# Low parts of the weights on VectorE, two attention tiles on the later path, and block 1 in two pieces for four triples

## The chip, the cores and the metric

One NeuronCore of one Trainium2 chip runs the kernel. The metric is the device time of one execution in microseconds (us); the median of three runs is compared. Engines: TensorE (PE; its weight loads are PEld), VectorE (DVE), ScalarE (ACT), GpSimd (POOL), SyncE (SP), which issues the transfers.

## The reference

Attention in chunks, then two gated layers over all 3072 tokens (4 batches of 768), all in float32 and with weights handed over as 64-bit floats:

```python
for c in range(768 // 32):            # 4 batches, 8 heads of 64
    k_full = concat(mem_k, k[:, :, max(0, 32*c - 16) : min(768, 32*c + 40)])
    a = softmax(q_c @ k_full.T / 8)   # up to 56 keys and 8 memory keys
    out[:, :, 32*c : 32*c + 32] = a @ v_full
x = out.transpose(0, 2, 1, 3).reshape(3072, 512)
x = (sigmoid(x @ w_gate) * (x @ w_val)) @ w_out        # d_ff 1536
h = x @ w_in; x = (h * sigmoid(1.702 * h)) @ w_out2    # d_ff 2048
```

## The kernel before, in words

**Products.** A float32 product is made of three products of reduced floats: every operand is kept as a high and a low part, and high x high, high x low and low x high are summed in PSUM. Tokens are worked in 6 blocks of 512. In the first layer d_ff is cut into 12 pieces f of 128; one triple is: the gate product (`first_product`: L727 with the high part of the weights and both parts of x, L734 with the low part of the weights), the value product in the same way, `gated()` (L751 sigmoid on ScalarE, L754 product on VectorE, L757 high part on ScalarE, L761 low part), and `gemm2` (L899) that adds the triple into the four output banks 4 to 7. A triple is 36 products of 512 columns, a block 432. The second layer does the same with L705. The low part of `gated` (L761) is on POOL in blocks 0 and 5 of the first layer, on VectorE in the others.

**Weights.** A piece of 128x512 weights arrives as 512 KB of 64-bit words and is made into high and low floats by `convert()`: load (SP), rebias (L258, ScalarE), rest (L263, VectorE: shifts the lower word in place), sign (L268 on ScalarE for even numbers, L272 on VectorE for odd ones), join (L277, VectorE), high (L282, ScalarE), low (L286, POOL). The first layer has 36 such pieces, kept for all blocks. Raw words lie in a ring of buffers `raw`, the joined words in a ring `f`.

**Attention.** A tile is 96 tokens of all 8 heads; there are 32 tiles. The first tiles (number below `NPE`, 11 here: tiles 0 to 5 before block 0, tiles 6 to 10 during block 0) take the TensorE path (`pe_path`): TensorE transposes queries (L379), keys (L387) and the normed weights (L586); scores are L496, the product with the values L646. VectorE takes maxima (L513), subtracts (L516), sums (L553) and inverts them (L555, L556); ScalarE takes exponentials (L524); the norm (L564) is split over VectorE and POOL. The result goes into x as high (L673) and low (L676) parts. Tiles from `NPE` on take the later path: queries and keys come in many small transfers and VectorE transposes them (L480; L483, L484, with copies L486), POOL and VectorE norm, VectorE transposes the weights in eight pieces (L621), and a tile's product with the values is issued together with the next tile's scores. The buffers of this path (`pb`) lie in the memory of `raw` 0 to 2 and `f` 0 and 1; so they are free only after the last conversion of the first 36.

**Order.** Every instruction is a task with an engine, an estimated duration and the things it reads and writes. The class `Schedule` plays the tasks through in time: an engine takes among its ready tasks the one due first. Products get their due time from a running clock, other tasks from what depends on them. The order found is written out as the program; each engine then runs its list strictly in order and waits on semaphores. A changed estimate can so change the order on every engine.

Of the kernel before, what the change touches and what calls it, by code (L numbers as in the profile page):

```python
# [8 lines left out]
F32 = mybir.dt.float32  # L9
# [22 lines left out]
class Schedule:  # L32
# [8 lines left out]
    def add(self, eng, dur, fn, r=(), w=(), table=None, nbytes=0, due=None, slack=0.0):  # L41
# [11 lines left out]
        for x in w:  # L53
# [4 lines left out]
            dict(eng=eng, dur=dur, fn=fn, deps=deps, table=table, nbytes=nbytes, due=due, slack=slack, succ=[])  # L58
# [11 lines left out]
    def run(self):  # L70
# [16 lines left out]
        while any(ready.values()):  # L87
# [20 lines left out]
            for s in t["succ"]:  # L108
# [3 lines left out]
                if not left[s]:  # L112
                    ready.setdefault(T[s]["eng"], []).append(s)
# [18 lines left out]
def kernel(  # L132
# [36 lines left out]
    NPE = NPRO + len(tiles[1])  # L169
# [33 lines left out]
    def xkeys(i):  # L203
        return [("x", i, c, o) for c in range(NCH) for o in range(2)]
# [27 lines left out]
    def convert(slot, src, gate=None):  # L232
# [31 lines left out]

        def sign():
# [26 lines left out]
        add("dve", 0.45, rest, r=[kr], w=[kr2])  # L292
        if u % 2:
# [42 lines left out]
    held_back = []  # L336
    SL = 0.5

    def attention(t, bufs, banks, pe_path, extra=None):
# [30 lines left out]

        if pe_path:
# [159 lines left out]
        if pe_path:  # L531
            tadd("pe", 1.32, pe_s, r=rs, w=[kb0, kb1])
# [35 lines left out]
        if pe_path:  # L568
# [6 lines left out]
            def ev_norm_m():  # L575
                norm(nc.gpsimd, T["pw"][:, :, TK:P], (0, TQ), (CTX, KW))

            en = ["dve", "dve" if early else "pool", "pool"]
            for c in range(NCK):
                tadd(en[c], 0.6 if en[c] == "dve" else 0.95, lambda c=c: ev_norm(c), r=ke + [kk["sm"]], w=[(kk["pw"], c)])  # L580
            tadd("pool", 0.3, ev_norm_m, r=ke + [kk["sm"]], w=[(kk["pw"], 3)])
# [16 lines left out]
            tadd("pe", 0.7, pe_pt, r=[(kk["pw"], c) for c in range(4)] + [bufs.kid], w=[kb0, kb1])  # L598
# [55 lines left out]
        def evict(part=None):  # L654

            g = range(t * NCK, (t + 1) * NCK)
            for i, blk in enumerate(sorted({c // NCH for c in g})):
# [7 lines left out]
                due = clock[0] - 3.0 * (NPRO - 1 - t) if t < NPRO and blk == 0 else None  # L665
# [18 lines left out]
        if pe_path:  # L684
            tadd("pe", 0.9, pe_pv, r=rp, w=[kb1])
            if t not in (NPRO - 1, NPE - 1):
# [33 lines left out]
    def first_product(slot, xb, n, bk, load=1.0):  # L720
        ts = [slice(t * P, (t + 1) * P) for t in range(NK)]

        def high():
            w = slots[slot]
            for t in range(NK):
                for x in (xhs, xls):
                    nc.tensor.matmul(  # L727
                        bank[bk][:, :n], w[:, 0, ts[t]], x[xb][:, t, :n], start=t == 0 and x is xhs, stop=False
                    )

        def low():
            w = slots[slot]
            for t in range(NK):
                nc.tensor.matmul(  # L734
                    bank[bk][:, :n], w[:, 1, ts[t]], xhs[xb][:, t, :n], start=False, stop=t == NK - 1
                )

        product(c_mm(n, 2 * NK), high, [("w", slot, 0)] + xkeys(xb), [("bank", bk)], load)
        product(c_mm(n, NK), low, [("w", slot, 1)] + xkeys(xb), [("bank", bk)], load)
# [110 lines left out]
    for u, (_, s, src) in enumerate(order):  # L850
        if u == 1:
            attend(tiles[0], lambda t: pro_bufs[t], lambda t: pro_banks[t])
        if u == NXR:
# [3 lines left out]
            attend(tiles[1], lambda t: pa, lambda t: (A0, A1))  # L857
# [227 lines left out]
```

## Time and profile before

| | us |
|---|---|
| median of three runs (lowest, highest) | 1235.61 (1234.24, 1237.63) |
| profiled execution, its span | 1238.0, 1236.2 |
| PE busy | 1201.4 (97%) |
| PEld busy | 983.8 (80%) |
| DVE busy | 625.0 (51%) |
| ACT busy | 474.4 (38%) |
| POOL busy | 232.5 (19%) |

The profile is of one execution, 2.4 us longer than the median; its span counts from the first to the last instruction. Busy shares are means over stages with different limits: the first 47.5 us load and make the first weights and tiles, then block 0 runs while the other weights are converted, then the blocks follow each other.

### The profile page before, as it was taken

What the parts mean: (1) busy time and instruction counts of PE and PEld (TensorE: products, weight loads), DVE (VectorE), ACT (ScalarE), POOL (GpSimd) and SP (SyncE); (2) the same over time, 40 slices, a digit from 0 to 9 for tenths busy, and PEclk for the clock granted to TensorE, in tenths of its full rate; (3) what the DMA queues carried; (4) which work ended last, traced back from release to release, by engine and by line L of the source; (5) the groups of instructions that cost most, each with busy time, mean ns of one, the idle gap of its engine ahead of it and who ended that gap; (6) DMA issues with size and microseconds to landing.
All of it is one profiled execution on the core that took longest, in us unless ns stands there. A gap on an engine that the chain in (4) does not pass through costs nothing.

```text
span 1236.2 us, 18066 instructions
## 1 busy us (share of the span) xinstructions
PE 1201.4 (97%) x7120; PEld 983.8 (80%) x7120; DVE 625.0 (51%) x1161; ACT 474.4 (38%) x754; POOL 232.5 (19%) x198
## 2 busy tenths in 40 slices
PE   6798899999999999999999999999999999999998
PEld 5676777888888888888888788888888888888887
DVE  7999851786488628826778621122322222322322
ACT  4688742343244314413576632232222222322222
POOL 2455640000000001000266652110010000100000
PEclk9799899999999999999999999999999999999999
DMA  9456423133022202400355420010100100100000
GB/s 225 142 160 183 138 55 72 33 58 71 16 54 50 67 9 49 97 3 18 120 179 159 147 69 1 17 51 1 42 26 1 63 8 1 68 1 1 35 1 35
DMA packets 166036, 78.03 MB, mean 63 GB/s; under 512 B 132542, under 2 KB 153278, under 8 KB 165950
## 3 DMA queue, kind: packets, MB, share of 16 engines
q1 hardware_dynamic: 165950, 76.87, 23.5%
q8 instruction: 56, 0.92, 0.3%
q14 instruction: 30, 0.25, 0.1%
HBM read 64.24 MB, written 12.58 MB: 62 GB/s over the span
## 4 chain that ended last, share of the span: by engine, by line
PE 79%; DVE 10%; DMA 4%; SPq 2%; issue 2%; POOL 2%; ACT 1%; DVEq 0%; POOLq 0%; ACTq 0%
PE bank L727 29%; PE bank L705 21%; PE bank L734 14%; PE bank L899 11%; DMA raw<-in_moe_w_out_dram 2%; DVE f L277 2%; SPq L306 2%; PE bank L646 2%; DVE raw L272 2%; PE bank L496 1%; DVE raw L263 1%; DVE raw_s L263 1%; DVE pw L564 1%; DMA raw<-in_moe_w_in_dram 1%; POOL w L286 1%
## 5 line engine op out<-in xcount | busy, mean ns | idle before, releaser
L727 PE MATMUL bank<-xh,w 128*128 128x512 f32 x960 | 376.8, 393 | 4.4 <-ACT sig L751 2.0
L727 PE MATMUL bank<-xl,w 128*128 128x512 f32 x960 | 375.2, 391 | 0.0
L754 DVE TENSOR_TENSOR sig<-bank,sig 128x512 f32<-128x512 f32 x168 | 115.9, 690 | 411.8 <-ACT sig L751 324.1
L734 PE MATMUL bank<-xh,w 128*128 128x512 f32 x960 | 257.4, 392 | 0.0
L751 ACT ACTIVATE sig<-bank 128x512 f32<-128x512 f32 x168 | 100.6, 599 | 369.2 <-PE bank L734 368.9
L705 PE MATMUL bank<-w,gh 128*128 128x512 f32 x768 | 236.4, 389 | 0.0
L727 PEld LDWEIGHTS bank<-xh,w 128*128 128x128 f32 x960 | 181.4, 189 | 45.2 <-ACT sig L751 3.7
L727 PEld LDWEIGHTS bank<-xl,w 128*128 128x128 f32 x960 | 181.4, 189 | 37.7
L734 PEld LDWEIGHTS bank<-xh,w 128*128 128x128 f32 x960 | 178.7, 188 | 37.5
L757 ACT ACTIVATE gh<-sig 128x512 fp32r<-128x512 f32 x168 | 106.1, 632 | 196.2 <-DVE sig L754 189.4
L705 PEld LDWEIGHTS bank<-w,gh 128*128 128x128 f32 x768 | 144.2, 188 | 29.8
L899 PE MATMUL bank<-gh,w 128*128 128x512 f32 x576 | 156.1, 393 | 0.6 <-DVE f L920 0.6
L705 PE MATMUL bank<-w,gl 128*128 128x512 f32 x384 | 149.4, 389 | 0.0
L761 DVE TENSOR_TENSOR gl<-sig,gh 128x512 fp32r<-128x512 f32 x128 | 91.0, 711 | 74.5 <-ACT gh L757 74.2
L899 PEld LDWEIGHTS bank<-gh,w 128*128 128x128 f32 x576 | 108.0, 189 | 24.1 <-DVE f L920 1.1
L286 POOL TENSOR_TENSOR w<-f,w 128x512 fp32r<-128x512 f32 x68 | 94.0, 1396 | 63.4 <-ACT w L282 62.1
L564 POOL TENSOR_TENSOR raw<-e,sm 96x448 f32<-96x448 f32 x21 | 21.6, 1030 | 401.3 <-DVE sm L556 401.3
L705 PEld LDWEIGHTS bank<-w,gl 128*128 128x128 f32 x384 | 72.1, 188 | 15.0
L948 POOL TENSOR_TENSOR xl<-f,xh 128x512 fp32r<-128x512 f32 x24 | 31.4, 1320 | 272.3 <-ACT xh L945 196.0
L899 PE MATMUL bank<-gl,w 128*128 128x512 f32 x288 | 78.1, 393 | 0.0
L621 DVE STREAM_TRANSPOSE pt<-raw 32x256 f32<-32x256 f32 x168 | 73.2, 436 | 2.6
L761 POOL TENSOR_TENSOR gl<-sig,gh 128x512 fp32r<-128x512 f32 x40 | 55.7, 1394 | 72.0 <-ACT gh L757 67.7
(84 smaller groups left out, 909.5 us busy)
## 6 DMA issues: line engine op xcount, KB each, us to landing
raw<-in_moe_w_out_dram SPq DMA_DIRECT2D x24, 512.0 KB
raw<-in_moe_w_in_dram SPq DMA_DIRECT2D x16, 512.0 KB
y_dram<-f SPq DMA_DIRECT2D x24, 256.0 KB
f<-y_dram SPq DMA_DIRECT2D x24, 256.0 KB
out_dram<-f SPq DMA_DIRECT2D x23, 256.0 KB
vn<-in_v_dram SPq DMA_DIRECT2D x24, 240.0 KB
raw<-in_moe_w_gate_dram SPq DMA_DIRECT2D x8, 512.0 KB
raw<-in_moe_w_val_dram SPq DMA_DIRECT2D x8, 512.0 KB
```

The source lines that it names most:

```text
L286: nc.gpsimd.tensor_tensor(out=w[:, 1, :], in0=ft, in1=w[:, 0, :].bitcast(F32), op=ALU.subtract)
L564: eng.tensor_tensor(out=dst, in0=e3()[r, :, c], in1=T["sm"][r].to_broadcast([n, H, keys[1] - keys[0]]), op=ALU.mult)
L621: nc.vector.transpose(T["pt"][r * CH : (r + 1) * CH, :, c * CH : (c + 1) * CH], T["pn"][c * CH : (c + 1) * CH, :, kb * CH : (kb + 1) * CH],)
L705: nc.tensor.matmul(ps_out, a, c, start=(first and i == 0 and j == 0), stop=(last and i == n - 1 and j == 2),)
L727: nc.tensor.matmul(bank[bk][:, :n], w[:, 0, ts[t]], x[xb][:, t, :n], start=t == 0 and x is xhs, stop=False)
L734: nc.tensor.matmul(bank[bk][:, :n], w[:, 1, ts[t]], xhs[xb][:, t, :n], start=False, stop=t == NK - 1)
L751: nc.scalar.activation(sig[:, :n], bank[src_sig][:, :n], AF.Sigmoid, scale=scale)
L754: nc.vector.tensor_tensor(out=sig[:, :n], in0=bank[src_val][:, :n], in1=sig[:, :n], op=ALU.mult)
L757: nc.scalar.activation(gh[:, :n], sig[:, :n], AF.Copy)
L761: eng.tensor_tensor(out=gl[:, :n], in0=sig[:, :n], in1=gh[:, :n].bitcast(F32), op=ALU.subtract)
L899: nc.tensor.matmul(bank[Y[m]][:, :n], w[:, wi, m * P : (m + 1) * P], g[:, :n], start=f == 0 and j == 0, stop=f == F1 - 1 and j == 2,)
L948: nc.gpsimd.tensor_tensor(out=xls[xb][:, m, :], in0=st[:, :BLK], in1=xhs[xb][:, m, :].bitcast(F32), op=ALU.subtract)
```

## The change

All low parts of weights are made on VectorE (`low_dve`). Of the conversions with even numbers rest and sign are both on VectorE, of the others both on ScalarE; for that there is a new form of rest, `rest_act`, which takes 16 bits of the lower word as a number and writes the shifted value as the bits of a float. In the TensorE path the middle piece of the norm and the memory part go to VectorE; the third piece stays on POOL. `NPE` becomes 9: tiles 9 and 10 take the later path, and the handling of tile 10's second part (`held_back`) goes. `SPLIT` makes block 1 run its first four triples on the first 352 tokens (to the end of tile 8), then the same four on the other 160, then the remaining eight whole. The low part of `gated` is on VectorE in all blocks of the first layer. Estimates of the planner change with it; MARGIN and SPREAD, which could move due times, are zero, and STEP is the 3.0 that stood there as a number.

```diff
-    NPE = NPRO + len(tiles[1])
+    NPE = NPRO + 3
...
+        low_dve = "d"[u % 1] == "d"
+        sign_on_dve = "da"[u % 2] == "d"
...
+        def rest_act():
+            half = bits().bitcast(U16).rearrange("p (c w) -> p c w", w=4)
+            nc.scalar.activation(
+                words()[:, :, 0].bitcast(F32), half[:, :, 1], AF.Copy, scale=7.5 * 2.0**-16, bias=2.0**23
+            )
...
-            nc.gpsimd.tensor_tensor(out=w[:, 1, :], in0=ft, in1=w[:, 0, :].bitcast(F32), op=ALU.subtract)
+            eng = nc.vector if low_dve else nc.gpsimd
+            eng.tensor_tensor(out=w[:, 1, :], in0=ft, in1=w[:, 0, :].bitcast(F32), op=ALU.subtract)
...
-        add("dve", 0.45, rest, r=[kr], w=[kr2])
-        if u % 2:
+        if "da"[u % 2] == "d":
+            add("dve", 0.42, rest, r=[kr], w=[kr2])
+        else:
+            add("act", c_act(512), rest_act, r=[kr], w=[kr2])
+        if sign_on_dve:
             add("dve", 0.9, sign_dve, r=[kr], w=[kr2])
         else:
             add("act", 1.4, sign, r=[kr], w=[kr2])
-        add("dve", 0.9, join, r=[kr, kr2], w=[kf])
+        add("dve", 0.7, join, r=[kr, kr2], w=[kf])
         add("act", c_act(512), high, r=[kf] + gate, w=[("w", slot, 0)])
-        add("pool", c_pool(512), low, r=[kf, ("w", slot, 0)], w=[("w", slot, 1)])
+        add(*(("dve", 0.7) if low_dve else ("pool", c_pool(512))), low, r=[kf, ("w", slot, 0)], w=[("w", slot, 1)])
...
+    STEP = 3.0
+    SPREAD = 0.0
+    MARGIN = 0.0
...
-                norm(nc.gpsimd, T["pw"][:, :, TK:P], (0, TQ), (CTX, KW))
-
-            en = ["dve", "dve" if early else "pool", "pool"]
+                norm(nc.vector, T["pw"][:, :, TK:P], (0, TQ), (CTX, KW))
+
+            en = ["dve", "dve", "pool"] if early else ["dve", "dve", "pool"]
...
-            attend(tiles[1], lambda t: pa, lambda t: (A0, A1))
+            attend(range(NPRO, NPE), lambda t: pa, lambda t: (A0, A1))
...
     def attention_b(b):
         for t in tiles[b]:
+            if t < NPE:
+                continue
...
-    def gemm2(b, f, i, n):
+    def gemm2(b, f, i, n, c0):
...
-                        bank[Y[m]][:, :n],
+                        bank[Y[m]][:, c0 : c0 + n],
                         w[:, wi, m * P : (m + 1) * P],
                         g[:, :n],
-                        start=f == 0 and j == 0,
+                        start=f == 0 and j == 0 and c0 == 0,
...
+    SPLIT = {1: (4, NPE * TQ - BLK)}
...
-        if 2 <= b + 1 < NB:
+        if b + 1 < NB:
             attention_b(b + 1)
...
-        for f in range(F1):
-            first_product(f, b % 2, n, G, LOAD)
-            i, tail = gated(n, G, 1.0, V, b == 0 or b == NB - 1)
-            first_product(F1 + f, b % 2, n, V, LOAD)
+
+        steps = [(f, 0, n) for f in range(F1)]
+        if b in SPLIT:
+            lead, c1 = SPLIT[b]
+            steps[:lead] = [(f, c, m) for c, m in ((0, c1), (c1, n - c1)) for f in range(lead)]
+        for f, c0, m in steps:
+            first_product(f, b % 2, m, G, LOAD, c0)
+            i, tail = gated(m, G, 1.0, V, False)
+            first_product(F1 + f, b % 2, m, V, LOAD, c0)
             tail()
             if pend:
                 gemm2(*pend)
-            pend = (b, f, i, n)
-        if b == 0:
-            held_back.pop()()
+            pend = (b, f, i, m, c0)
```

Three places show how the order moves. Lines of the changed program have other numbers: L267 is rest, L284 sign, L289 join, L299 low, L780 the product of `gated`; L517 scores, L667 the product with the values, L753 the first product, L928 `gemm2`.

First, VectorE (DVE) some 80 instructions into the program, when the first weights are ready and block 0 begins. Before it reads:

```order
L263 TENSOR_SCALAR raw0_74<-raw0_74 128x512
L277 SCALAR_TENSOR_TENSOR f0_77<-f0_77,xl1_raw_91 128x512
L272 TENSOR_SCALAR raw0_74<-raw0_74 128x512
L263 TENSOR_SCALAR raw_s3_656<-raw_s3_656 128x512
L277 SCALAR_TENSOR_TENSOR f1_78<-f1_78,raw0_74 128x512
L754 TENSOR_TENSOR sig0_82<-bank1_67,sig0_82 128x512
L263 TENSOR_SCALAR raw1_75<-raw1_75 128x512
```

After:

```order
L299 TENSOR_TENSOR w0_100<-f0_77,w0_100 128x512
L267 TENSOR_SCALAR raw2_76<-raw2_76 128x512
L299 TENSOR_TENSOR w12_101<-f1_78,w12_101 128x512
L284 TENSOR_SCALAR raw2_76<-raw2_76 128x512
L289 SCALAR_TENSOR_TENSOR f3_80<-f3_80,xh1_raw_90 128x512
L289 SCALAR_TENSOR_TENSOR f2_79<-f2_79,raw2_76 128x512
L267 TENSOR_SCALAR xl1_raw_91<-xl1_raw_91 128x512
L267 TENSOR_SCALAR raw_s3_661<-raw_s3_661 128x512
```

The low parts (L299) of the first weights now stand in VectorE's list between the rests and joins; two rests and a join that stood ahead of the first product come behind it.

Second, TensorE (PE) where tile 10's result is due. Before, tile 10's weights are transposed and multiplied with the values between two whole products of block 0's last triples (w23 and w34), and block 1 begins with 512 columns:

```order
L727 MATMUL bank1_67<-xl0_89,w23_1483 128x512
L734 MATMUL bank1_67<-xh0_88,w23_1483 128x512 x4
L586 MATMUL bank2_68<-ident_a_660,pw_a_659 128x96 x4
L586 MATMUL bank3_69<-ident_a_660,pw_a_659 128x96 x4
L646 MATMUL bank3_69<-pt_98,vn_92 64x96 x8
L899 MATMUL bank4_70<-gh0_84,w34_1770 128x512
```

After, tile 10's product with the values and tile 11's scores stand in block 1, directly ahead of the first product of 160 columns, which reads what tiles 9 and 10 give:

```order
L928 MATMUL bank7_73<-gl1_87,w27_642 128x352
L667 MATMUL bank2_68<-pt_98,vn_92 64x96 x4
L667 MATMUL bank3_69<-pt_98,vn_92 64x96 x4
L517 MATMUL bank2_68<-kt_94,qt_93 32x64
...
L753 MATMUL bank0_66<-xh1_727,w0_100 128x160
L753 MATMUL bank0_66<-xl1_728,w0_100 128x160
```

576 of the kernel's products, 144 of them with 352 columns in place of 512, stand ahead of that L667; tile 9's stands 48 products earlier in the same way. Tile 8's scores stand behind 368 products of block 0.

Third, VectorE's list for tile 9, which took the TensorE path before. The tile that closed block 0's attention before (tile 10) read:

```order
L553 TENSOR_REDUCE sm_97<-e_95 96x8
L555 TENSOR_SCALAR sm_97<-sm_97 96x8
L556 RECIPROCAL sm_97<-sm_97 96x8
L564 TENSOR_TENSOR pw_a_659<-e_95,sm_97 32x8x56
L754 TENSOR_TENSOR sig1_83<-bank1_67,sig1_83 128x512
L594 COPY pt_98<-bank3_69 128x384
```

Tile 9 reads now:

```order
L574 TENSOR_REDUCE sm_97<-e_95 96x8
L504 STREAM_TRANSPOSE kt_94<-raw1_75 128x12x32
L505 STREAM_TRANSPOSE kt_94<-raw1_75 128x12x32
L507 COPY kt_94<-f1_78 128x4x8 x3
L576 TENSOR_SCALAR sm_97<-sm_97 96x8
L577 RECIPROCAL sm_97<-sm_97 96x8
L780 TENSOR_TENSOR sig0_82<-bank1_67,sig0_82 128x352
L585 TENSOR_TENSOR raw2_76<-e_95,sm_97 64x8x8
L585 TENSOR_TENSOR raw2_76<-e_95,sm_97 32x8x8
L787 TENSOR_TENSOR gl1_87<-sig1_83,gh1_85 128x352
L642 STREAM_TRANSPOSE pt_98<-raw2_76 32x8x32 x8
L501 STREAM_TRANSPOSE qt_93<-f0_77 128x384
```

The key transposes (L504, L505) are those of tile 10, from `raw1`; they stand ahead of tile 9's inverse, norms and weight transposes (L642). On SP's list the transfers for these two tiles come in this order behind the last load of weights: 3 of queries, 4 of memory keys, 16 of keys into `raw0`, 9 of queries, 16 of keys into `raw1`. Before, 1, 4, 16, 11 and then the next 16.

## Rows read from the trace of the kernel before

**Rows 1.** Windows: from:to us, length, busy us (instructions) of PE, PEld, DVE, ACT, POOL; PEclk, DMA share, GB/s.

```profile
47.50:163.00 115.50, 105.50 (x702) 83.84 (x702) 104.95 (x138) 91.57 (x144) 72.87 (x58) 0.96 0.58 172
214.29:1232.30 1018.01, 1016.48 (x5665) 835.29 (x5663) 466.11 (x912) 345.38 (x538) 136.22 (x105) 1.00 0.17 46
600.00:720.00 120.00, 118.69 (x533) 97.00 (x532) 86.95 (x112) 79.87 (x121) 71.85 (x51) 1.00 0.48 151
```

**Rows 2.** The chain of waits, 715 to 735 us: start, us, what.

```profile
723.67 1.81 PE bank L727 x8
```

**Rows 3.** Timeline at 47.5 us: start, us, engine, line, operation, out<-in, shape, count, idle before.

```profile
47.51 0.80 PE L727 MATMUL bank<-xh,w 128*128 128x512 f32 x1 [2.03 <-ACT w L282]
47.54 2.79 POOL L286 TENSOR_TENSOR w<-f,w 128x512 fp32r<-128x512 f32 x2 [0.39 <-ACT w L282]
47.67 1.51 DVE L263 TENSOR_SCALAR xh_raw<-xh_raw 128x512 int32<-128x512 int32 x1
```

**Rows 4.** Timeline of PE, 211 to 233 us.

```profile
214.29 0.39 PE L727 MATMUL bank<-xh,w 128*128 128x512 f32 x1
...
216.19 0.74 PE L496 MATMUL bank<-kt,qt 64*32 64x64 f32 x48
...
230.70 0.88 PE L646 MATMUL bank<-pt,vn 128*64 128x96 f32 x16
...
232.18 1.20 PE L734 MATMUL bank<-xh,w 128*128 128x512 f32 x4
```

**Rows 5.** Timeline at 139 us, PE.

```profile
139.59 0.60 PE L387 MATMUL bank<-ident_a,qkn_a 128*128 128x128 f32 x4
...
139.94 0.47 PE L727 MATMUL bank<-xh,w 128*128 128x512 f32 x1
```

**Rows 6.** Timeline of DVE where POOL is idle or has just begun.

```profile
127.12 0.68 DVE L277 SCALAR_TENSOR_TENSOR f<-f,raw 128x512 int32<-128x512 int32 x1
...
135.31 0.75 DVE L272 TENSOR_SCALAR raw_s<-raw_s 128x512 uint16<-128x512 uint16 x1
...
137.08 0.42 DVE L263 TENSOR_SCALAR raw<-raw 128x512 int32<-128x512 int32 x1
```

**Rows 7.** Windows, line L263 alone: from:to, length, DVE busy us (instructions).

```profile
47.50:163.00 115.50, 33.06 (x33) 0.96 0.58 172
```

**Rows 8.** Windows, line L272 alone.

```profile
47.50:163.00 115.50, 23.51 (x17) 0.96 0.58 172
```

**Rows 9.** Windows, line L277 alone.

```profile
47.50:163.00 115.50, 31.20 (x33) 0.96 0.58 172
```

**Rows 10.** Groups of POOL, 47.5 to 163 us: busy us, mean ns, idle before.

```profile
L286 POOL TENSOR_TENSOR w<-f,w 128x512 fp32r<-128x512 f32 x34 | 46.8, 1390 | 34.0 <-ACT w L282 33.9
```

**Rows 11.** Timeline of SP, 160 to 179 us: issues of transfers.

```profile
161.25 0.32 SPq L306 DMA_DIRECT2D f<-in_q_dram  x1
...
171.90 5.18 SPq L306 DMA_DIRECT2D f<-in_q_dram  x11
177.18 1.84 SPq L306 DMA_DIRECT2D raw<-in_k_dram  x4
```

**Rows 12.** Groups of ACT, 47.5 to 163 us.

```profile
L268 ACT ACTIVATE raw<-raw 128x512 f16<-128x512 f32 x10 | 13.7, 1374 | 0.0
L258 ACT ACTIVATE f<-raw 128x512 f32<-128x512 f32 x21 | 13.7, 677 | 0.0
```

**Rows 13.** Timelines of DVE, 177 to 184 and 214 to 228 us.

```profile
178.45 0.58 DVE L480 STREAM_TRANSPOSE qt<-f 128x384 f32<-128x384 f32 x1 [2.10 <-DMA f<-in_q_dram]
...
218.87 0.56 DVE L483 STREAM_TRANSPOSE kt<-raw 128x384 f32<-128x384 f32 x1
...
220.74 0.64 DVE L553 TENSOR_REDUCE sm<-e 96x8 f32<-96x512 f32 x1
...
227.25 0.69 DVE L754 TENSOR_TENSOR sig<-bank,sig 128x512 f32<-128x512 f32 x1 [0.19 <-PE bank L734]
```

**Rows 14.** The page's costliest groups.

```profile
L727 PEld LDWEIGHTS bank<-xh,w 128*128 128x128 f32 x960 | 181.4, 189 | 45.2 <-ACT sig L751 3.7
```

More of the change, by code (lines that the diff above doesn't have):

```diff
@@ L39, in __init__, with add @@
         self.writer, self.readers = {}, {}
-    def add(self, eng, dur, fn, r=(), w=(), table=None, nbytes=0, due=None, slack=0.0):
+    def add(self, eng, dur, fn, r=(), w=(), table=None, nbytes=0, due=None, slack=0.0, margin=0.0):
         i = len(self.tasks)
@@ L57, in add @@
         self.tasks.append(
-            dict(eng=eng, dur=dur, fn=fn, deps=deps, table=table, nbytes=nbytes, due=due, slack=slack, succ=[])
+            dict(eng=eng, dur=dur, fn=fn, deps=deps, table=table, nbytes=nbytes, due=due, slack=slack, margin=margin, succ=[])
         )
@@ L201, in open_x1, with xkeys @@
             xs.append(cp.tile([P, NK, BLK], F32R, tag=f"{x}1", name=f"{x}1"))
-    def xkeys(i):
-        return [("x", i, c, o) for c in range(NCH) for o in range(2)]
+    def xkeys(i, c0=0, n=BLK):
+        return [("x", i, c, o) for c in range(c0 // CH, (c0 + n) // CH) for o in range(2)]
     NW = 3 * F1
@@ L369, in attention @@
         kvn = [(kk["vn"], i) for i in range(4)]
+        mg = MARGIN if t >= NPRO else 0.0
         if pe_path:
@@ L596, in ev_pt @@
                     nc.scalar.activation(dst, src, AF.Copy)
-            tadd("pe", 0.7, pe_pt, r=[(kk["pw"], c) for c in range(4)] + [bufs.kid], w=[kb0, kb1])
+            tadd("pe", 0.7, pe_pt, r=[(kk["pw"], c) for c in range(4)] + [bufs.kid], w=[kb0, kb1], margin=mg)
             tadd("act", c_act(384), lambda: ev_pt(0), r=[kb0], w=[(kk["pt"], 0)])
@@ L664, in evict @@
                 xb = blk % 2
-                due = clock[0] - 3.0 * (NPRO - 1 - t) if t < NPRO and blk == 0 else None
+                due = None
+                if t < NPRO and blk == 0:
+                    due = clock[0] - STEP * (NPRO - 1 - t)
+                elif t < NPE and blk <= 1 and SPREAD:
+                    due = clock[0] + SPREAD * (t - NPRO + 1) / (NPE - NPRO)
                 for o, (bk, kb, c0, p0, n) in enumerate(outs):
@@ L684, in attention @@
         if pe_path:
-            tadd("pe", 0.9, pe_pv, r=rp, w=[kb1])
-            if t not in (NPRO - 1, NPE - 1):
+            tadd("pe", 0.9, pe_pv, r=rp, w=[kb1], margin=mg)
+            if t < NPRO - 1 or t >= NPRO:
                 evict()
@@ L718, in product, with first_product @@
         clock[0] += dur * load
-    def first_product(slot, xb, n, bk, load=1.0):
+    def first_product(slot, xb, n, bk, load=1.0, c0=0):
         ts = [slice(t * P, (t + 1) * P) for t in range(NK)]
@@ L734, in low @@
                 nc.tensor.matmul(
-                    bank[bk][:, :n], w[:, 1, ts[t]], xhs[xb][:, t, :n], start=False, stop=t == NK - 1
+                    bank[bk][:, :n], w[:, 1, ts[t]], xhs[xb][:, t, c0 : c0 + n], start=False, stop=t == NK - 1
                 )
-        product(c_mm(n, 2 * NK), high, [("w", slot, 0)] + xkeys(xb), [("bank", bk)], load)
-        product(c_mm(n, NK), low, [("w", slot, 1)] + xkeys(xb), [("bank", bk)], load)
+        product(c_mm(n, 2 * NK), high, [("w", slot, 0)] + xkeys(xb, c0, n), [("bank", bk)], load)
+        product(c_mm(n, NK), low, [("w", slot, 1)] + xkeys(xb, c0, n), [("bank", bk)], load)
     ng = [0]
```

11 lines of the change are left out of this document (6 added, 5 removed).

## The prediction

> **What bounds the kernel now.** I first split the span into stretches with the windows view [rows 1]. From 214.29 us to the end TensorE is busy 1016.5 of 1018.0 us at full granted clock: there only TensorE's own work counts, and an edit that lets another engine work less saves nothing. The stretch 47.5 to 163 differs: VectorE is busy 104.95 of 115.5 us, TensorE 105.5, and the granted clock is 0.96. So what can be won lies ahead of 214.29.
>
> The chain gives TensorE's rate: 8 products of 512 columns in 1.81 us, 226.7 ns each [rows 2]. The first product starts at 47.51 [rows 3]. By the order of the code 576 products (12 triples of block 0 and the first 4 of block 1, 36 each) stand ahead of the one that starts at 214.29 [rows 4]. They need 576 x 0.2267 = 130.6 us. In the same stretch stand the TensorE parts of five attention tiles. The 4 transposes of keys of such a tile take 0.35 us (139.59 to 139.94) [rows 5]; the 4 of queries and the 8 of weights I count at the same 0.09 each, 1.4 for all 16; the product with the values and the next tile's scores take 1.48 (230.70 to 232.18) [rows 4]. That makes 2.9 a tile, 14.5 for five. 47.5 + 130.6 + 14.5 = 192.6, so TensorE loses 21.7 us before 214.29. This is the pool from which the change can draw.
>
> Why it loses them is seen on VectorE. At 47.67 a "rest" (L263) takes 1.51 us beside a POOL "low" [rows 3]; alone it takes 0.42, a "sign" (L272) 0.75, a "join" (L277) 0.68 [rows 6]. Over the stretch these three take 33.06, 23.51 and 31.20 us for 33, 17 and 33 [rows 7 to 9]; at the lone durations they would take 13.9, 12.8 and 22.4. So VectorE spends 38.7 us of its 105 waiting beside POOL, whose 34 lows take 46.8 us [rows 10]. The weights come late because of that, and behind them the later tiles, whose buffers are those of the conversions.
>
> **VectorE's work up to the last conversion.** Without the three lines 105.0 - 87.8 = 17.2 us are left. The change adds 34 lows and 10 gated low parts (L761), which nothing shows on VectorE in this stretch but the same shape does elsewhere: a join, also 128x512 with two inputs, takes 0.68; so 44 x 0.68 = 29.9. Joins stay, 33 x 0.68 = 22.4. Rests and signs of the odd half go to ScalarE: 17 x 0.42 + 17 x 0.75 = 19.9. The norms of three tiles come over (about 0.8 a tile, an estimate from the size ratio of 448 and 64 to 512 columns), and one tile's work leaves: nothing together. Sum 17.2 + 29.9 + 22.4 + 19.9 = 89.4, 15.6 less than now.
>
> The first transfer of the later tiles, which needs the conversions' buffers, starts at 161.25 [rows 11], 113.7 us after the first product. With VectorE as idle as now, 113.7 x 89.4 / 105.0 = 96.8; two rests and a join that the order moves behind the first product add 1.6: 145.9. TensorE sets a second bound: by the new order tile 8's scores stand behind 368 products and two tiles, 47.5 + 83.4 + 5.8 + 0.7 = 137.4, and VectorE has some ten rows (two maxima, two subtractions, a join, rest, sign, two lows, a sum: 6 us) to the last low that frees a buffer, 144.
>
> ScalarE sets a third. It is busy 91.57 of 115.5 us [rows 1]. Up to that transfer it will have one tile less (an exponential, its table loads, copies, about 4 us) and two sets of query and key copies less (3.5), both estimates by the rebias's row for like sizes, and gains 16 rests of a form that no row shows. The nearest rows are the rebias (L258, f32 to f32, 0.677) and the sign (L268, into 16 bits, 1.374) [rows 12]. The new rest writes 32-bit words, as the rebias does: I take 0.68, 16 x 0.68 = 10.9, together 95 us. Never idle it would be done at 142.5, and as idle as VectorE is now (105.0 of 115.5) at 152. Between the three bounds I take **147 us** for that first transfer.
>
> **The chain that two tiles now form.** Tiles 9 and 10 no longer run ahead of the conversions' end but behind it, and the 160-column products of block 1 stand behind both. From the first transfer on:
> - 32 small transfers, then 16 of tile 10's keys, stand on SP's queue. Now 21 take 10.65 us (161.25 to 171.90) and 11 take 5.28 [rows 11]: 15.9, and 16 more at 0.51, 8.2; the last lands about 1.3 after its issue (177.18 to 178.45) [rows 11, 13]. 25.4 us.
> - VectorE's order puts tile 10's key transposes ahead of tile 9's sums and norms, so tile 9 waits for tile 10's keys. From such key transposes to the last transposed weights it is 218.87 to 227.25, 8.4 us, less the sum (0.64) that is done before: 7.7 [rows 13].
> - Tile 9's product with the values, about 0.8. Then tile 10 from its scores (216.19 for tile 11) to its last transposes (227.25): 11.1 [rows 4, 13].
> - Its product with the values and tile 11's scores 1.5; two maxima, high and low parts of x 1.5.
>
> Sum 25.4 + 7.7 + 0.8 + 11.1 + 1.5 + 1.5 = 48.0; 147 + 48.0 = **195.0** for the first 160-column product. TensorE's own work up to there is 47.5 + 97.9 (432 products) + 8.7 (three tiles) + 23.0 (144 products of 352 columns) + 3.6 = 180.7, so the split does not cover the chain fully; 14 us of waiting are left, and I expect them at tile 9's and tile 10's values.
>
> **What the split costs.** 512 columns at the higher level, 2.4 GHz, are 213.3 ns of the 226.7; 13.4 are left over per product. 352 columns then cost 160 ns and 144 of them 23.0 us; 160 columns cost 80, 11.5 us. But 4 products of 128 columns take 0.35 us, 88 each [rows 5]; scaled by columns, 110 for 160. A single weight load lasts 189 ns [rows 14], though it overlaps the products. I take 110, between 80 and 189: 15.8 us. Short products also leave the gating of each triple less cover; 0.7 us for that.
>
> A rule speaks against this part: the Trainium skill, "TensorE: Matmul & The Clock Gate", section "LDWEIGHTS (loading the stationary operand)", makes a weight load cost by its columns alone, P/1.2 ns, 107 for 128, however few columns stream behind it. By it 144 products cost 15.4 us and not 11.5. The row with 88 for 128 columns is nearer to it than to proportion.
>
> **Behind it.** Lows of the later weights and block 5's gated low parts move to VectorE too. From 600 to 720 us VectorE is busy 86.95 and TensorE 118.69 of 120 [rows 1]: TensorE's work hides it, at 0, with 1.3 us to win there and, were the cover gone, some 2 to lose. MARGIN and SPREAD are 0 and add nothing.
>
> **The sum.** 195.0 + 15.8 + 0.7 = 211.5 for the point that now lies at 214.29, plus tile 11's scores (0.7) that the new order has ahead of it: 215.0. So 3.5 us less. The profiled execution took 1238.0 us (span 1236.2), 2.4 above the median of 1235.61; after: 1234.5 in a profiled execution like it, **1232** in the median. One microsecond on the first transfer is one on the end; it breaks even at 150.5.
>
> **Rivals.**
> - Quicker (1222 to 1228). The 160-column products at 80 ns give 4.3 us, transfers at the 0.46 us of the last four on SP [rows 11] 2.3, a first transfer at TensorE's bound of 144 us 3.0: together 9.6 more, 1222.5. For it: VectorE's new work would fit into 89 us. Against: three things at once.
> - Eaten up (1235 to 1239.3). ScalarE becomes the bound of the conversions and is as idle as VectorE is now: first transfer at 152, 1.5 us lost, 1237. For it: it alternates with VectorE several times a conversion. Against: TensorE's own pace leaves it time in this stretch, and the lows, which VectorE now does at half the time, no longer lag.
> - Short products dear (about 1243). If each waits for its weight load, 144 x 0.189 = 27.2 us, 11.4 more than summed: 8 us slower than now. It decides from 134 ns on. Against: the 88 ns row.
> - Chain late (over 1239.3). Tiles 9 and 10 stand behind the conversions; if the first transfer comes after 154 us, the move of two tiles costs more than lows on VectorE give. A rest of 1.374 on ScalarE does it: 106 us, 153.5 without any idle time and 164 as idle as VectorE is now, 1238 to 1249. So would lows on VectorE if what slows it weren't POOL: 30 us on top of 105. Against the first stands the rebias's row, against the second the same instruction with 0.42 and 1.51.
>
> **How the numbers follow.** 0.3% (3.7 us) is about what a measurement of this kernel tells from no change. The forecast's own case, first transfer at 143 to 150 us, gives 1228 to 1235: 0.48, of which 0.30 lie under 1231.9, since the bounds of VectorE and TensorE lie below 147. Quicker 0.19. Eaten up 0.13, of which 0.03 slower. Short products dear 0.07. Chain late 0.13. So faster 0.30 + 0.19 = 0.49; same 0.18 + 0.10 = 0.28; slower 0.23. The range runs from the sum of the favourable bounds, 1222, to the dear short products, 1243; about 0.1 lie outside, nearly all above. The forecast's own range is 1228 to 1235.
>
> **What would show it.** VectorE in block 0: rests and signs at 0.42 and 0.75 nearly throughout, no POOL lows. The first transfer of tile 9's queries near 147 us (143 to 150). TensorE waiting for the transposed weights of tiles 9 and 10, some 14 us in all. The first 160-column product near 195, starts 110 ns apart. From 211.5 on TensorE as full as now. The prediction is wrong if ScalarE's rest takes over 1 us, if the first transfer comes after 150 us, or if 160-column products lie over 134 ns apart.

## The result, and the profile after

The changed kernel takes 1248.37 us (median of 4, 1247.98 to 1248.49) against 1235.3 us before (there too of 4): ratio 1.0107, 95% interval 1.009 to 1.0125. It is 13 us slower; forecast were 1232 us and a range of 1222 to 1243.

The windows view of the changed kernel, with the columns of [rows 1], shows where:

```profile
47.50:163.00 115.50, 110.21 (x675) 89.72 (x674) 90.51 (x172) 95.06 (x151) 5.12 (x10) 0.97 0.53 158
163.00:195.44 32.44, 27.67 (x311) 25.34 (x310) 23.01 (x60) 10.36 (x18) 1.87 (x2) 0.95 0.38 75
195.44:222.87 27.43, 26.82 (x124) 26.61 (x125) 11.60 (x34) 4.73 (x13) 0.93 (x1) 0.50 0.28 46
...
600.00:720.00 120.00, 120.00 (x598) 98.67 (x597) 88.47 (x156) 88.22 (x138) 6.12 (x5) 1.00 0.49 156
```

In the first stretch, block 0 in the main, VectorE is busy 90.5 us where it was 105.0, POOL 5.1 where it was 72.9, and TensorE 110.2 where it was 105.5 [rows 1]. So far the change does what it says. The third row is the loss: for 27.43 us TensorE is busy but for one wait of 0.61, at a granted clock of 0.50. These are the products of 160 columns, called the short products from here on; those of 512 columns are the wide ones. The timeline of TensorE, first at two places ahead of them where it waits, then around them:

```profile
147.03 0.79 PE L753 MATMUL bank<-xh,w 128*128 128x512 f32 x1 [4.32 <-ACT sig L777]
...
180.35 0.88 PE L667 MATMUL bank<-pt,vn 128*64 128x96 f32 x16 [1.63 <-issue]
...
188.97 0.80 PE L928 MATMUL bank<-gl,w 128*128 128x352 f32 x4
192.47 1.55 PE L667 MATMUL bank<-pt,vn 128*64 128x96 f32 x16 [2.70 <-DVE pt L642]
193.95 1.09 PE L517 MATMUL bank<-kt,qt 64*32 64x64 f32 x48
195.44 0.50 PE L753 MATMUL bank<-xh,w 128*128 128x160 f32 x1 [0.40 <-ACT xh L699]
196.55 0.50 PE L753 MATMUL bank<-xl,w 128*128 128x160 f32 x1 [0.61 <-DVE xl L702]
...
199.19 0.41 PE L753 MATMUL bank<-xl,w 128*128 128x160 f32 x1
199.41 0.41 PE L753 MATMUL bank<-xh,w 128*128 128x160 f32 x1
...
222.87 0.71 PE L753 MATMUL bank<-xh,w 128*128 128x512 f32 x1
...
226.37 0.70 PE L928 MATMUL bank<-gh,w 128*128 128x160 f32 x4
...
227.87 0.57 PE L928 MATMUL bank<-gl,w 128*128 128x160 f32 x4
228.27 0.43 PE L753 MATMUL bank<-xh,w 128*128 128x512 f32 x1
```

TensorE waits 2.70 us for tile 10's transposed weights and 1.0 for its x; behind that the short products start 0.213 us apart (199.19, 199.41) and do so to the end of the run. TensorE's weight loads (PEld) are as busy as its products, 26.61 of the 27.43 us. Eight wide products from 222.87 on still take 3.50 us in place of 1.81, 0.44 each (by proportion 160 columns would take 0.14 at this clock, an estimate, and not 0.213); then the clock is back: the four short products at 227.87 take 0.40 together, 0.10 each. 124 short products lie in the third row, 26.8 us without the wait; the 20 behind, in fours between wide ones, take 2.1. So the 144 cost 29.0 us, where the forecast had 16.5 (15.8 and 0.7 for gating).

The forecast's other places came out near. The first transfer of the later tiles, on SP:

```profile
144.79 1.28 SPq L322 DMA_DIRECT2D f<-in_q_dram  x3
```

144.79 us, between the bound of 144 and the 147 taken; and the first short product at 195.44 (forecast 195). The chain between the two took 50.7 us where 48.0 were summed and started 2.2 earlier: that its end came out to 0.4 us is in part luck. VectorE's and ScalarE's groups from 45 to 160 us answer to [rows 6, 12]:

```profile
L299 DVE TENSOR_TENSOR w<-f,w 128x512 fp32r<-128x512 f32 x36 | 24.7, 691 | 4.3 <-ACT w L294 4.1
L289 DVE SCALAR_TENSOR_TENSOR f<-f,raw 128x512 int32<-128x512 int32 x23 | 15.5, 682 | 0.6 <-ACT raw L280 0.5
L284 DVE TENSOR_SCALAR raw<-raw 128x512 uint16<-128x512 uint16 x11 | 8.3, 753 | 0.0
L267 DVE TENSOR_SCALAR raw<-raw 128x512 int32<-128x512 int32 x11 | 5.0, 458 | 0.6 <-DMA raw<-in_moe_w_val_dram 0.6
...
L273 ACT ACTIVATE raw<-raw 128x512 f32<-128x512 uint16 x11 | 7.4, 672 | 0.6 <-DMA raw<-in_moe_w_gate_dram 0.4 <-DMA raw<-in_moe_w_out_dram 0.3
```

Rest, sign and join stand at 0.46, 0.75 and 0.68 on VectorE, the low part at 0.69, ScalarE's new rest at 0.67: the durations summed in the prediction.

### The profile page after: what moved, and what is told of

The parts are those of the page before. It is cut to its first block, busy times and chain, and to the rows that moved or that the text cites. A ratio compares the mean times of both kernels' runs of the same rounds, so it can differ in the third digit from the quotient of the medians.

```text
span 1245.9 us, 18295 instructions
## 1 busy us (share of the span) xinstructions
PE 1216.2 (98%) x7232; PEld 1006.8 (81%) x7232; DVE 617.3 (50%) x1270; ACT 487.6 (39%) x787; POOL 90.7 (7%) x90
## 4 chain that ended last, share of the span: by engine, by line
PE 92%; SPq 3%; DVE 2%; ACT 1%; issue 1%; DMA 1%; POOL 0%; DVEq 0%; POOLq 0%; ACTq 0%
PE bank L753 34%; PE bank L731 21%; PE bank L760 17%; PE bank L928 15%; SPq L322 3%; PE bank L667 2%; PE bank L517 1%; DVE pw L585 1%; PE bank L607 1%; PE bank L400 0%; PE bank L408 0%; DMA raw<-in_moe_w_gate_dram 0%; DVE pt L642 0%; DVE sm L574 0%; ACT raw L280 0%
## 5 line engine op out<-in xcount | busy, mean ns | idle before, releaser
L753 PE MATMUL bank<-xh,w 128*128 128x512 f32 (+2 forms) x992 | 387.9, 391 | 6.3 <-ACT sig L777 5.5
L753 PE MATMUL bank<-xl,w 128*128 128x512 f32 (+2 forms) x992 | 386.7, 390 | 0.6 <-DVE xl L702 0.6
L780 DVE TENSOR_TENSOR sig<-bank,sig 128x512 f32<-128x512 f32 (+2 forms) x172 | 116.7, 678 | 432.1 <-ACT sig L777 326.6
L760 PE MATMUL bank<-xh,w 128*128 128x512 f32 (+2 forms) x992 | 262.9, 390 | 0.0
L777 ACT ACTIVATE sig<-bank 128x512 f32<-128x512 f32 (+2 forms) x172 | 101.5, 590 | 395.0 <-PE bank L760 394.5
L753 PEld LDWEIGHTS bank<-xh,w 128*128 128x128 f32 x992 | 192.0, 194 | 45.2 <-ACT sig L777 7.1
L753 PEld LDWEIGHTS bank<-xl,w 128*128 128x128 f32 x992 | 192.1, 194 | 37.3 <-DVE xl L702 0.8
L783 ACT ACTIVATE gh<-sig 128x512 fp32r<-128x512 f32 (+2 forms) x172 | 106.9, 621 | 194.6 <-DVE sig L780 186.6
L928 PE MATMUL bank<-gh,w 128*128 128x512 f32 (+2 forms) x608 | 158.7, 386 | 0.0
L787 DVE TENSOR_TENSOR gl<-sig,gh 128x512 fp32r<-128x512 f32 (+2 forms) x156 | 108.4, 695 | 79.7 <-ACT gh L783 79.1
L928 PEld LDWEIGHTS bank<-gh,w 128*128 128x128 f32 x608 | 113.6, 193 | 21.7
L642 DVE STREAM_TRANSPOSE pt<-raw 32x256 f32<-32x256 f32 x184 | 80.1, 435 | 3.7 <-POOL raw L585 1.0
L928 PE MATMUL bank<-gl,w 128*128 128x512 f32 (+2 forms) x304 | 80.2, 386 | 0.0
L928 PEld LDWEIGHTS bank<-gl,w 128*128 128x128 f32 x304 | 56.2, 192 | 10.9
L299 DVE TENSOR_TENSOR w<-f,w 128x512 fp32r<-128x512 f32 x68 | 47.2, 704 | 10.6 <-ACT w L294 7.7
```

The source lines that it names most:

```text
L299: eng.tensor_tensor(out=w[:, 1, :], in0=ft, in1=w[:, 0, :].bitcast(F32), op=ALU.subtract)
L642: nc.vector.transpose(T["pt"][r * CH : (r + 1) * CH, :, c * CH : (c + 1) * CH], T["pn"][c * CH : (c + 1) * CH, :, kb * CH : (kb + 1) * CH],)
L753: nc.tensor.matmul(bank[bk][:, :n], w[:, 0, ts[t]], x[xb][:, t, c0 : c0 + n], start=t == 0 and x is xhs, stop=False)
L760: nc.tensor.matmul(bank[bk][:, :n], w[:, 1, ts[t]], xhs[xb][:, t, c0 : c0 + n], start=False, stop=t == NK - 1)
L777: nc.scalar.activation(sig[:, :n], bank[src_sig][:, :n], AF.Sigmoid, scale=scale)
L780: nc.vector.tensor_tensor(out=sig[:, :n], in0=bank[src_val][:, :n], in1=sig[:, :n], op=ALU.mult)
```

## The experiments

The theory after the result: the conversions' part gains time; the split loses it, because a wait ahead of the short products takes TensorE's clock down and short products leave it there. The rivals: short products lower the clock by themselves; each waits for its weight load, 190 ns or more, at any clock; the conversions' part gains nothing. Each kernel is timed beside the kernel before (1236.0 to 1236.7 us in these jobs).

**The conversions' part alone.** From the changed kernel:

```diff
-    NPE = NPRO + 3
+    NPE = NPRO + len(tiles[1])
-    SPLIT = {1: (4, NPE * TQ - BLK)}
+    SPLIT = {}
```

and tile 10's held-back second part as before. 

> The change's part on VectorE and ScalarE alone: low parts on VectorE, rest and sign in pairs, norms and gated low parts on VectorE; tiles 9 and 10 stay on the TensorE path and block 1 runs whole. Theory (the lows cost nothing there, the split does): TensorE starts near 45 us, block 0 loses some 8 to 10 us in place of some 20, so 1220 to 1227 us. Rival (the conversions themselves gain nothing by it): 1232 us or more.

Measured: 1219.8 us, ratio 0.9864 (0.9848 to 0.9881), 16 us faster than before. The window from 45 to 160 us, and the two longest of TensorE's waits from 40 to 260:

```profile
45.00:160.00 115.00, 111.59 (x811) 89.60 (x812) 101.35 (x193) 106.47 (x171) 9.25 (x15) 1.00 0.60 174
```

```profile
PE bank L753 <- ACT w L294: 1.4, 1, 1.4
PE bank L928 <- ACT w L294: 1.2, 1, 1.2
```

TensorE is busy 111.6 of 115 us at full clock. The product that started at 214.29 starts at 197.67. By the prediction's sum (45.27 for the first product + 130.6 + 14.5 = 190.4) 7.3 of the 21.7 us lost before are still lost; 3.1 of them are waits, the longest 1.4. This half gains 16 us where the forecast had 3.5 for the whole change, and this kernel is the fastest of all.

**The other half alone.** Conversions and gated low parts as before, later path and split as changed:

```diff
-        low_dve = "d"[u % 1] == "d"
+        low_dve = False
-        if "da"[u % 2] == "d":
+        if True:
-            i, tail = gated(m, G, 1.0, V, False)
+            i, tail = gated(m, G, 1.0, V, b == 0 or b == NB - 1)
```

and signs in turn as before. 

> The other half alone: tiles 9 and 10 on the later path and block 1 split, with conversions as before (lows and gated low parts of blocks 0 and 5 on POOL). Theory (the chain starts with the end of the conversions): first transfer of tile 9 near 161 us in place of 145, first 160-column product near 211, 14 to 18 us more than the changed kernel, about 1264. Rival (the start of the chain doesn't hang on the conversions' pace): within 3 us of the changed kernel, 1248.

Measured: 1257.46 us (ratio 1.0176, 1.0161 to 1.0191), 9 us above the changed kernel; the theory's 1264 is missed, and its mechanism too: the first transfer comes at 146.39, not 161. What moved it from 161 to 145 is above all that three tiles in place of five stand ahead of it: with five it starts at 154.66 to 163.40 in all kernels here that keep them (before 161.25), with three at 139.16 to 146.39, whether the lows are on POOL or not; how the conversions are done moves it by 1.6 us between this kernel and the changed one. The first short product starts at 200.37, 5 us later than in the changed kernel. No wait over 0.6 us stands directly ahead of it, and the short products run 0.11 us apart. Then they make TensorE wait themselves: 1.29 us for a sigmoid (to 204.46), behind which they still start 0.11 apart, and 2.12 us for its product; behind that they are 0.213 apart:

```profile
208.24 0.50 PE L753 MATMUL bank<-xh,w 128*128 128x160 f32 x1 [2.12 <-DVE sig L780]
208.53 0.41 PE L753 MATMUL bank<-xl,w 128*128 128x160 f32 x1
208.75 0.41 PE L753 MATMUL bank<-xh,w 128*128 128x160 f32 x1
```

**The split where nothing waits.** The same split in block 3 as well:

```diff
-    SPLIT = {1: (4, NPE * TQ - BLK)}
+    SPLIT = {1: (4, NPE * TQ - BLK), 3: (4, NPE * TQ - BLK)}
```

> The changed kernel with the same split of the first four triples in block 3 too, where no wait stands ahead of the products of 160 columns. Theory A (the granted clock falls by the wait ahead of them in block 1, and short products only don't bring it back): in block 3 they lie 102 ns apart at full clock, 23.0 + 14.7 in place of 32.6 us, 5 us more than the changed kernel, about 1253.5. Theory B (short products take the clock down by themselves): they fall to 213 ns apart with a granted clock of 0.5 in block 3, 21 us more, about 1269. Theory C (each short product waits for its weight load): 190 to 213 ns at full clock, 18 to 21 us more.

Measured: 1255.99 us (ratio to the kernel before 1.0159, 1.0144 to 1.0174), 7.6 more than the changed kernel. Block 3's short products in the windows view and TensorE's timeline:

```profile
431.00:447.00 16.00, 15.39 (x132) 15.01 (x132) 10.49 (x31) 5.53 (x11) 0.93 (x1) 1.00 0.37 69
```

```profile
438.83 0.28 PE L753 MATMUL bank<-xl,w 128*128 128x160 f32 x1
438.94 0.28 PE L753 MATMUL bank<-xh,w 128*128 128x160 f32 x1
```

Full clock through 16 us of them, 0.11 us apart, though a wait of 0.6 stands among them. So short products don't lower the clock by themselves, and their weight loads cost no 189 ns each: theories B and C fall. Theory A's 5 us were too few: the products lie 0.113 apart and not 0.102, 16.1 us for all 144, and 0.6 us of wait come to it. That is 23.0 + 16.1 + 0.6 - 32.6 = 7.1.

**The same with a wait put ahead.** In block 3 the first short product is made to wait for 16 small VectorE instructions that add zero times the last gated low part to x:

```diff
+        last = None
         for f, c0, m in steps:
+            if b == 3 and c0 and f == 0:
+                def hold(i=last, c0=c0):
+                    for _ in range(4):
+                        for t in range(NK):
+                            x = xls[b % 2][:, t, c0:]
+                            nc.vector.scalar_tensor_tensor(
+                                out=x, in0=gls[i][:, : BLK - c0].bitcast(F32), scalar=0.0, in1=x.bitcast(F32), op0=ALU.mult, op1=ALU.add
+                            )
+                add("dve", 4.0, hold, r=[("gl", last)], w=xkeys(b % 2, c0, m))
...
+            last = i
```

> The kernel with the split in blocks 1 and 3, and in block 3 a wait put ahead of the first product of 160 columns: VectorE adds zero times the last gated low part to those columns of x, four times over, 16 small instructions, so that TensorE stands still for some 4 us. Theory A (the wait takes the clock down and short products don't bring it back): granted clock 0.5 and 213 ns through block 3's short products, 4 us of wait and 14 to 15 of low clock more than with the split alone in both blocks (1255.99): 1273 to 1276. Rival (something else in block 1 keeps the clock down): the clock is back within some 3 us, 1260 to 1263.

Measured: 1270.16 us, 14.2 more than without the wait. TensorE's waits from 430 to 462 us, its timeline where the clock falls, and the rest of block 3's short products:

```profile
PE bank L753 <- DVE xl L1007: 2.0, 1, 2.0
PE bank L753 <- ACT sig L777: 1.3, 1, 1.3
```

```profile
441.19 0.27 PE L753 MATMUL bank<-xl,w 128*128 128x160 f32 x1
441.30 0.28 PE L753 MATMUL bank<-xh,w 128*128 128x160 f32 x1
...
441.72 0.42 PE L753 MATMUL bank<-xl,w 128*128 128x160 f32 x1
441.93 0.41 PE L753 MATMUL bank<-xh,w 128*128 128x160 f32 x1
```

```profile
447.40:460.30 12.90, 12.90 (x63) 12.90 (x62) 1.30 (x4) 0.84 (x3) 0.00 (x0) 0.50 0.00 0
```

The wait was 2.0 us (to 435.55), not 4, with 1.3 more at a sigmoid (to 439.67), which the run above has with 0.6. Directly behind both the products still start 0.11 us apart; the clock falls at some 441.5, in the middle of the run, 1.9 us behind the second wait and with no gap of TensorE there, and stays at 0.50 to the run's end. So the two waits together are enough; which of them would do alone wasn't tried. 2.7 us more of waiting than in the run above gave 14.2 us. This is the loss of the changed kernel, made at will in another block.

**Wide products between.** The steps of block 1 in another order:

```diff
-            steps[:lead] = [(f, c, m) for c, m in ((0, c1), (c1, n - c1)) for f in range(lead)]
+            head = [(f, 0, c1) for f in range(lead)]
+            mixed = [x for f in range(lead) for x in ((f, c1, n - c1), (lead + f, 0, n))]
+            steps = head + mixed + steps[2 * lead :]
```

> The changed kernel with the order of block 1's steps changed: behind the four triples on 352 tokens come in turn one on 160 tokens and one whole (triples 4 to 7). Only the first 36 short products then run without wide ones between. If the low clock behind the wait is what makes the 160-column products dear, and wide products bring it back: 36 products at 213 ns, the other 108 near 102, 12 us less than the changed kernel, 1235 to 1238. If short products are dear by their weight loads whatever the clock: 1247 to 1249, as the changed kernel.

Measured: 1237.91 us (ratio 1.0014, 1.0005 to 1.0024), 10.5 less than the changed kernel. Behind the same waits:

```profile
189.00:201.60 12.60, 8.94 (x94) 7.96 (x93) 8.78 (x26) 3.11 (x7) 0.93 (x1) 0.64 0.35 61
201.60:207.50 5.90, 5.90 (x18) 4.69 (x18) 4.60 (x11) 0.34 (x1) 0.00 (x0) 0.61 0.24 36
207.50:240.00 32.50, 32.11 (x254) 28.27 (x252) 11.84 (x30) 8.54 (x16) 0.93 (x1) 1.00 0.24 50
```

The second row holds wide products only: the clock comes back among them, and the short ones behind, in the third row, run at full clock.

**Another width.** `SPLIT = {1: (4, 256)}`. 

> The changed kernel with block 1 cut at 256 in place of 352: the lead has 144 products of 256 columns, the second pieces 256 columns too. The lead covers 5.7 us less, so TensorE waits longer at tile 10. If only very short products fail to bring the clock back: 256 columns do it within a few us, the second pieces take some 20 us in place of 29, 1238 to 1242. If 256 columns don't either: 213 to 240 ns each at a granted clock of 0.5, 31 to 35 us, 1250 to 1256.

Measured: 1234.76 us (ratio 0.9984, 0.9972 to 0.9996), 3.2 less than the least that was expected. TensorE waits 1.4, 1.8 and 1.3 us between 185 and 200. The timeline of the first second pieces, behind the waits of 1.4 and 1.8, and the windows:

```profile
195.24 0.41 PE L753 MATMUL bank<-xl,w 128*128 128x256 f32 x1
195.45 0.41 PE L753 MATMUL bank<-xh,w 128*128 128x256 f32 x1
...
196.41 0.27 PE L753 MATMUL bank<-xl,w 128*128 128x256 f32 x1
196.52 0.28 PE L753 MATMUL bank<-xh,w 128*128 128x256 f32 x1
```

```profile
187.00:199.70 12.70, 8.87 (x101) 7.77 (x101) 9.33 (x29) 3.61 (x8) 0.93 (x1) 0.73 0.34 60
199.70:212.30 12.60, 12.60 (x105) 12.60 (x106) 6.66 (x16) 2.41 (x6) 0.00 (x0) 1.00 0.28 44
```

The clock is low when the second pieces begin (0.21 us apart), and some 2 us later it is back (0.12 apart), with no wide product in between; the wait of 1.3 us behind that doesn't lower it again. A run of 160 columns stayed low for 27 us, one of 256 came back. At the lower clock both widths lie 0.21 us apart, so the columns don't set that pace; the weight load, the same for both, would, but no run shows it by itself.

**A longer lead.** `SPLIT = {1: (6, NPE * TQ - BLK)}`. 

> The changed kernel with six triples in the lead of block 1 in place of four: 72 more products of 352 columns (11.5 us) stand between tile 9's scores and the first product of 160 columns, and 216 short products in place of 144. Theory A (a wait of TensorE takes the clock down, short products keep it where it is): the 3.7 us of waiting at tile 10 go, the short products stay near 111 ns at full clock, about 24 us for 216; 3.3 us more for the longer split, some 15 less for the clock, 4 less for the wait: 1232 to 1236. Theory B (long runs of short products take the clock down): 213 ns, 216 of them 46 us, about 1258 to 1262.

Measured: median 1245.68 of ten executions, not the 1232 to 1236 of theory A; but two of the ten took 1231.13 and 1232.82, with a mean granted clock of 0.990 and 0.987 where the others have 0.976 to 0.979. In the profiled one (1245.82) the wait at tile 10 is still 2.3 us, but the short products start 0.11 us apart behind it; at its first triples the short run makes waits of its own. TensorE's waits from 190 to 240 us and the window behind the last of them:

```profile
PE bank L753 <- DVE sig L780: 2.4, 1, 2.4
PE bank L667 <- DVE pt L642: 2.3, 1, 2.3
PE bank L753 <- ACT sig L777: 1.3, 1, 1.3
```

```profile
206.00:236.00 30.00, 29.82 (x140) 29.82 (x140) 6.45 (x18) 2.67 (x9) 0.00 (x0) 0.50 0.13 20
```

30 us at 0.50 lower the mean clock of 1244 us by 0.012, an estimate: that is the distance between the two groups. So one and the same program falls or, as far as its mean clock tells, doesn't fall, and 14 us hang on it. Theory A is right on the clock and was wrong on the waits: I had priced the missing cover of short triples at 0.7 us; here it makes 3.7, and brings the clock down.

**No split.** `SPLIT = {}`, tiles 9 and 10 still late. 

> The changed kernel without the split: tiles 9 and 10 on the later path, block 1 whole. Theory (the chain of the two late tiles ends near 195 us whatever TensorE does): TensorE stands still for 20 us or more before block 1, then runs its 144 products with 512 columns in 32.6 us where the changed kernel took some 30 with short products at the low clock; so about as long as the changed kernel, 1245 to 1252. Rival (the split made the chain late by VectorE's and ScalarE's extra gating): 1240 or less.

Measured: 1245.03 us, 3.3 less than the changed kernel. TensorE waits 9.1 us for tile 10's weights, not 20, since block 0 itself lost 8.1 in two waits at earlier tiles' weights; block 1's first product that needs tiles 9 and 10 starts at 188.68 in place of 195.44, and the first transfer at 139.16 in place of 144.79. So the chain does not end near 195 whatever TensorE does; what moved its start wasn't tried. The split as it stands is worth less than nothing, and the late tiles without it lose 25.2 us against the fastest kernel (1219.8), more than the 16.2 that the conversions' part gains.

**What of the conversions gains.** Three kernels put one part of the fastest back, `low_dve = False`: 

> The lows-alone kernel (1219.8) with only the low parts of the weights put back on POOL; rest and sign in pairs, norms and gated low parts stay on VectorE and ScalarE. Theory (the wait of VectorE beside POOL's lows is what the change takes away): rests, signs and joins take two times as long or more beside them, TensorE loses 10 us or more again: 1229 to 1236. Rival (the pairing of rest and sign or the gated low parts bring it): 1219 to 1224.

Measured: 1227.12 us, 7.3 more, between the theory's range and the rival's. VectorE's groups (45 to 160 us) beside POOL's lows: join, norm and sign are longer again (0.68, 0.73 and 0.76 in the fastest kernel), but by 1.2 to 1.4 times and not by two:

```profile
L289 DVE SCALAR_TENSOR_TENSOR f<-f,raw 128x512 int32<-128x512 int32 x19 | 15.6, 825 | 0.0
L585 DVE TENSOR_TENSOR pw_a<-e,sm 32x448 f32<-32x448 f32 (+1 forms) x15 | 15.3, 1017 | 0.4
L284 DVE TENSOR_SCALAR raw<-raw 128x512 uint16<-128x512 uint16 x11 | 10.4, 950 | 0.3
```

4.2 us of TensorE's waiting stand here at one sigmoid, so not all of the 7.3 need be VectorE's slower work; the order moved too, and the two weren't told apart.

Rests all on VectorE, signs in turn: 

> The lows-alone kernel (1219.8) with rest and sign shared out as before the change: all rests on VectorE, signs in turn on ScalarE and VectorE; lows stay on VectorE. VectorE gets 16 rests (6.7 us) and ScalarE loses them (10.9). Theory (POOL's lows were the cost, the pairing matters little): within 4 us, 1219 to 1224. Rival (VectorE, busy 101 of 115 us in that stretch, is the bound now): 1226 or more.

Measured: 1220.4 us, 0.6 more: this can't be told from nothing.

Gated low parts of blocks 0 and 5 on POOL: 

> The lows-alone kernel (1219.8) with the gated low parts of blocks 0 and 5 back on POOL, as before the change. 12 instructions of 1.39 us on POOL beside VectorE's rests and joins in block 0: they hold VectorE some 8 to 12 us, less than TensorE's cover there: 1220 to 1224. Rival (they don't touch VectorE): 1219 to 1220.

Measured: 1222.39 us, 2.6 more, with a profiled execution at 1220.43; small at most.

All three back at once, so that only the norms on VectorE and the planner's estimates differ from the kernel before: 

> The lows-alone kernel with all of its moved work but the norms put back (lows and gated low parts on POOL, rest and sign as before): what is left against the kernel before is the norms of the TensorE path on VectorE and the planner's new estimates. If the parts add up (lows 7.3, gated low parts 2.6, pairing 0.6 of the 16.2 us), it stands some 5 to 6 us under the kernel before: 1229 to 1232. If norms and estimates are worth nothing by themselves: 1234 to 1238.

Measured: 1230.84 us (ratio 0.9948, 0.9929 to 0.9967), 5.6 less than before. The parts add up: 7.3 + 0.6 + 2.6 + 5.6 = 16.1 of 16.2. That it comes out to 0.1 is luck, since 0.6 and 2.6 are hardly clear of the noise. How the 5.6 fall to norms and to estimates wasn't tried.

## Why the prediction was wrong

**The step that failed** is in "What the split costs": "I take 110, between 80 and 189: 15.8 us". The 110 was right as far as it goes: at full clock, in block 3, the 144 short products took 16.1 us and 0.6 of waiting, where the forecast had 15.8 and 0.7. By the Trainium skill, "TensorE: Matmul & The Clock Gate", section "LDWEIGHTS (loading the stationary operand)", a weight load costs P/1.2 ns by its columns alone, 107 ns for 128. The 0.11 of a run at full clock agree; at the lower clock the products of a run lie 0.213 apart, twice as much, for which the section has no figure. But the step priced every short product at the full clock, although the chain, one paragraph above, put 14 us of waiting ahead of them, and the trace of before shows what a wait does. Its TensorE at 130 us:

```profile
130.09 1.54 PE L586 MATMUL bank<-ident_a,pw_a 96*128 96x96 f32 x8 [3.68 <-POOL pw_a L564]
...
133.19 0.63 PE L727 MATMUL bank<-xh,w 128*128 128x512 f32 x1
133.62 0.63 PE L727 MATMUL bank<-xl,w 128*128 128x512 f32 x1
```

Behind the wait of 3.68 us wide products start 0.43 us apart in place of 0.227; such stretches make the granted clock of 0.96 in [rows 1]. That short products would stay there for 27 us no row of before shows: what was to be read was the fall. In the changed kernel the 144 products took 29.0 us, 12.5 more than the 16.5 of the forecast. The first of them came 0.4 us late and the second waited 0.6; the first eight wide products behind cost 1.7 more; TensorE won the 1.3 us that it could in 600 to 720. 12.5 + 0.4 + 0.6 + 1.7 - 1.3 = 13.9; the profiled execution was forecast at 1234.5 and took 1247.98, 13.5 above. The 0.7 us for gating held in block 3 only: in two of the kernels above the short products made 3.4 and 3.7 us of waiting themselves, and the clock fell behind it.

**What held.** That the time is won or lost ahead of 214 us; the durations on VectorE and ScalarE; the first transfer; the chain's end at 195, in part by luck; the bound of 134 ns for a short product as the point that decides. The waits near the short products were 1.6, 2.7 and 1.0 us, 5.3 and not 14, since TensorE came later too: block 0 lost 4.3 us at a sigmoid (142.7 to 147.0, behind table loads and signs in ScalarE's list) and ran at the low clock for its next eight products.

**The rivals.** "Short products dear" had the right place and side, and half of the mechanism: not a load of 189 ns at any clock, but a pace of 0.11 us that the lower clock doubles. Its price, 1243, was therefore 5 us short. "Eaten up" did not come true: ScalarE did not hold up the first transfer. But it worked without a gap from 136 to 147 us, and the 4.3 us at the sigmoid are its doing.

**What was credited wrongly.** "The weights come late because of that, and behind them the later tiles": with lows on POOL and three tiles in block 0 the first transfer came at 146.39. Putting the lows back on POOL costs 7.3 us; the start of the later tiles was set more by the two tiles that stood ahead of it. So two halves were summed as one gain: the conversions alone gain 16.2 us, and the later path with the split then loses 28.6, in the two profiled executions 28.1. Rows give 27.6 of these: the split triples 23.0 + 29.0 - 32.6 = 19.4, of them 12.9 by the clock (29.0 for 16.1); the waits 5.3; the sigmoid's wait with the low clock behind it 6.1; another at 52 us 1.0; the first wide products 1.7; less 2.8 for two tiles off the TensorE path and 3.1 for the waits of the faster kernel in the same stretch.

## What to carry to other kernels

Where a wait of a few us is left ahead of short products, or they make one themselves, price them at the lower clock for the whole run, unless wide products come first; look for the wait in the same sum that makes the products short. Put wide work behind a wait (here a 512-column triple), or cut so that the pieces stay wide: 256 columns recovered here, 160 didn't, and widths between weren't tried. And time the halves of a change apart: one half here was worth 16 us and the other more than ate it.

## What the runs showed of the hardware

TensorE can be busy without a gap for 26 us and stay at the lower of its two clocks (granted 0.50, 1.2 GHz): 160-column products, 0.213 us apart. The same products at full clock are 0.11 apart and stay so (16 us in block 3), even over a wait of 0.6 us; waits of 2.0 and 1.3 us among the first of them took the clock down, 1.9 us after the second had ended. Products of 256 columns, at 0.21 us too at the lower clock, came back to the full one within some 2 us, where they are 0.12 apart. Near the edge it differs from execution to execution: one program took 1231 to 1233 us twice and 1244 to 1247 eight times.
